# One store of eight PSUM banks for all stages, and a planner that knows of the port that VectorE and GpSimd share: a Fourier mixing layer followed by a SoLU layer on one core

## The chip, the cores and the metric

The kernel runs on one core of one Trainium2 chip. The metric is the device time of one execution in microseconds, as the median of the runs shown. The engines are called PE (TensorE), DVE (VectorE), ACT (ScalarE), POOL (GpSimd) and SP (SyncE, which issues the DMAs).

## What is computed

The input `x` has 8 images of 3136 tokens with 256 features. The first half mixes the tokens by a Fourier transform along the tokens, a complex 256x256 product with soft thresholding at 0.01, and the inverse transform. The second half takes the 25088 resulting tokens through a layer with 1024 hidden features:

```python
X = np.fft.rfft(x, axis=1)
Yr = Xr @ w_r - Xi @ w_i + b_r
Yi = Xr @ w_i + Xi @ w_r + b_i
Yr = np.sign(Yr) * np.maximum(np.abs(Yr) - lam, 0.0)
Yi = np.sign(Yi) * np.maximum(np.abs(Yi) - lam, 0.0)
y = np.fft.irfft(Y, n=x.shape[1], axis=1)
...
h = x @ w_in
e = np.exp(h - h_max)
sm = e / (np.sum(e, axis=-1, keepdims=True) + 1e-09)
solu = h * sm
ln = (solu - mu) / np.sqrt(var + 1e-06) * g_ln
return (ln @ w_out).astype(np.float32)
```

Each fp32 product is made of three fp16 products (a high and a low half of each side).

## The kernel before, in words

**The front, for each image.** 3136 tokens are 98 x 32, and the transform is done in two steps. `fwd1` (L549; `fwd1_first` at L574 for image 0) reads `x` in eight chunks `xt`, splits each into `xh` (ACT) and `xl` (DVE), multiplies by the 98-point matrix and writes `av` to DRAM. Ahead of it `load_peak` (L501) reads the image once more and takes its largest absolute value on DVE (`peaks`). `fwd2` (L626) does the 32-point step for 13 units and splits the result into `Xh` and `Xl`. `mix` (L714) multiplies by the weights (`yt`), clips (`yc`, on DVE), subtracts (`y`, on POOL) and splits again (`yh` on ACT, `yl` on POOL). `inv1` (L735) and `inv2` (L783) go back, through DRAM, into a ring of tokens in SBUF, `ring_hi` and `ring_lo`.

**The layer, for each of 196 tiles of 128 tokens.** `moe_head` (L816) makes two halves of 512 hidden features. Each half is six matmuls into one PSUM bank `ph`, whose maximum DVE takes (`nm`). From both maxima come the short columns `m`, `c` and `ch`; then ACT writes `u`, the exponential of `ph`, and DVE multiplies it by `ph` in place (also a row `u`). That last row frees the bank. POOL adds up the sums (`se`, `total`, `a`). `moe_turn` (L860) splits `u` into `lh` (ACT) and `ll` (POOL), has both transposed by DMA into `th` and `tl`, and forms the factor `r` in three POOL steps from ACT's sum of squares (`junk`). `moe_tail` (L880) multiplies `th` and `tl` by `wout` into one bank `po`; ACT scales it by `r` into `o`, which frees the bank, and one to three DMAs write `o` out.

**PSUM.** The eight banks are split into three pools (L427 to L429): three banks `ph` for heads, one bank `po` for tails, four banks `pf` for the front. Only image 0's front may use all, in a fixed turn by `front_psum` (L433), and some tiles of the last image borrow a `pf` bank (`spare`).

**What sets the order.** The kernel records every operation in a `Plan` (L222), with its engine, what it needs and a key that says which stage is due first. `weigh` (L281) gives each operation a length from constants (L228 to L231). `order` (L314) then runs through the program: for each engine it takes, among the operations that can start first, the one with the smallest key, and notes when the engine is free and when a PSUM or SBUF buffer comes free (`may_start`, L334). The order that comes out is the one in which each engine gets its instructions; on the chip they run in that order, with semaphores. The stages of one image's tiles are planned beside `front_a` (`load_peak` and `fwd1`) of the next-but-one image and `front_b` (`fwd2`, `mix`, `inv1`) of the next. As the plan records everything, all instructions carry one source line, L312.

Of the kernel before, what the change touches and what calls it, by code (L numbers as in the profile page):

```python
# [12 lines left out]
F32 = mybir.dt.float32  # L13
# [84 lines left out]
class View:  # L98
# [3 lines left out]
    def __init__(self, tile, rows, cells, dtype, path=()):  # L102
        self.tile, self.rows, self.cells, self.dtype, self.path = tile, rows, cells, dtype, path
# [61 lines left out]
class Tile:  # L165


    def __init__(self, pool, kind, shape, dtype, kw):
        self.pool, self.kind, self.shape, self.dtype, self.kw = pool, kind, shape, dtype, kw
        self.ap, self.writes, self.reads, self.users, self.owner = None, [], [], set(), None  # L170
# [20 lines left out]
class Kind:  # L191


    def __init__(self, bufs, free):
        self.bufs, self.free, self.placed, self.freed = bufs, free, [], []


class Pool:
    def __init__(self, pool, bufs, dram=False, free=False):
        self.pool, self.bufs, self.dram, self.free, self.kinds = pool, bufs, dram, free, {}  # L200

    def tile(self, shape, dtype, name, bufs=None):
        kind = self.kinds.setdefault(name, Kind(bufs or self.bufs, self.free))
        t = Tile(self.pool, kind, shape, dtype, dict(name=name, **({"bufs": bufs} if bufs else {})))
        if self.dram:
            return DramView(t)
        return View(t, (0, shape[0]), np.arange(int(np.prod(shape[1:]))).reshape(shape[1:]), dtype)


class Op:  # L210
    def __init__(self, engine, key, seq):
        self.engine, self.key, self.seq = engine, key, seq
        self.calls, self.length, self.moved, self.tiles = [], 0.0, 0.0, []
        self.needs, self.next, self.start, self.end, self.half = set(), [], None, None, False

# [6 lines left out]
class Plan:  # L222
# [91 lines left out]
    def order(self):  # L314
        ready = {e: [] for e in self.ENGINES}
        free = dict.fromkeys(self.ENGINES, 0.0)
        waits, bus, half = {}, 0.0, False
        for op in self.ops:
# [9 lines left out]
        for t, op in sorted(((t, min(t.users, key=lambda op: op.seq)) for t in left), key=lambda x: (x[1].key, x[1].seq)):  # L328
            if not t.kind.free:
                turn[t] = turns.get(t.kind, 0)  # L330
                turns[t.kind] = turn[t] + 1
        done = []

        def may_start(op):  # L334
            at = max(free[op.engine], op.at)
            for t in op.tiles:
                if t.owner is None:
                    k = t.kind
                    if turn.get(t, len(k.placed)) != len(k.placed):
                        return np.inf  # L340
                    n = len(k.placed) - k.bufs
                    if n >= 0:
                        at = max(at, k.freed[n] if n < len(k.freed) else np.inf)
            return at

        while len(done) < len(self.ops):
# [19 lines left out]
            op.start = at  # L366
            op.end = free[e] = at + op.length
            if op.moved:
                bus = max(bus, op.end) + op.moved
                op.end = bus + 2000.0  # L370
            for t in op.tiles:
                if t.owner is None:
                    t.owner = op
                    t.kind.placed.append(t)
                left[t] -= 1
                if not left[t]:
                    insort(t.kind.freed, max(o.end + self.SEEN[o.engine] for o in t.users))
            for o in op.next:
# [29 lines left out]
def fft_mix_solu_kernel(ctx: ExitStack, tc, x, w_r, w_i, b_r, b_i, w_in, w_out, g_ln, fa, fa16, fb, fs, gb, gs, ia, out):  # L408
# [22 lines left out]
    turns = [0]  # L431

    def front_psum(b):  # L433

        pool, name = ps_f, "pf"
        if b == 0:
            turns[0] += 1
            if turns[0] % 8 == 0:
                pool, name = ps_o, "po"
            elif turns[0] % 2 == 0:  # L440
                pool, name = ps_h, "ph"
        return pool.tile([P, HF], F32, name=name)

# [339 lines left out]
    def inv2(b, g):  # L783
# [5 lines left out]
        for eh in range(ND):  # L789
            pa = ps_f.tile([P, HF], F32, name="pf")  # L790
            nc.reserve(*(ring[:, eh, to : to + z - a] for ring in (ring_hi, ring_lo) for a, z, to in ((0, first, j0), (first, n, 0)) if z > a))
# [23 lines left out]

    def moe_head(k, spare):  # L816
        j = (2 * k[0] * S + k[1] * P) % R
# [3 lines left out]
        for h in range(2):  # L821
            cs = slice(h * HF, (h + 1) * HF)
            p = ps_f.tile([P, HF], F32, name="pf") if spare else ps_h.tile([P, HF], F32, name="ph")
            n = 0
            with nc.together():
                for dh in range(ND):
                    for lh, rh in ((hi, win_hi), (hi, win_lo), (lo, win_low)):
                        nc.tensor.matmul(p, lh[:, dh], rh[:, dh, cs], start=n == 0, stop=n == 3 * ND - 1)
                        n += 1
            m = sp.tile([P, 1], F32, name="nm")  # L830
            nc.vector.tensor_reduce(m, p, AX.X, ALU.max, negate=True)
            ph.append(p)
            nm.append(m)
# [45 lines left out]

    def moe_tail(k, parts, r, spare=False):  # L880
# [22 lines left out]

    pw = ps_o.tile([P, HF], F32, name="po")
    with nc.together():
# [95 lines left out]
    def power_of_two(peaks, un, sc, k):  # L1001

        top = sp.tile([P, 1], F32, name="wpeak", bufs=2)
        nc.vector.tensor_reduce(top, peaks, AX.X, ALU.max)
        pw = ps_f.tile([P, HF], F32, name="pf")
        nc.tensor.transpose(pw[:1, :P], top, ident)
# [3 lines left out]
        nc.vector.tensor_scalar(top.bitcast(U32), top.bitcast(U32), 0x7F800000, None, ALU.bitwise_and)  # L1010
        pw = ps_f.tile([P, HF], F32, name="pf")
        nc.tensor.matmul(pw[:, :1], ones[:1], top, start=True, stop=True)
# [15 lines left out]
    def finish_w_out(wo_s):  # L1028
# [10 lines left out]
        for half in wo_s[2:]:  # L1039
            nc.vector.tensor_tensor(total, total, half, op=ALU.add)  # L1040
        pw = ps_f.tile([P, HF], F32, name="pf")
        with nc.together():
# [51 lines left out]
    for b in range(B):  # L1094
# [9 lines left out]
        for n, t in enumerate(tiles):  # L1104
            need = min((t + 1) * P - (b % 2) * S, S)
            while groups < N2 // G2 and groups * G2 * N1 < need:
                nc.key = first + n - 2
                inv2(b, groups)
                groups += 1

            nc.key = first + n
            heads.append(moe_head((b // 2, t), b == B - 1 and n == 0))
# [3 lines left out]
            moe_tail(*turned.pop(0), b == B - 1 and n > L - 3 and n % 2 == 0)  # L1116
        while groups < N2 // G2:
# [28 lines left out]
```

## Time and profile before

| | us |
|---|---|
| median of 3 runs | 1732.97 |
| lowest and highest run | 1728.72, 1737.52 |
| the profiled execution, whole | 1739.42 |
| its span, first to last instruction | 1737.6 |

The mean granted clock of TensorE over the span is 0.974. The page gives each engine's busy time and its share of the span. In the tables of windows each row is a stretch of 100 us, with the busy time and the count of instructions of PE, PE's weight loads, DVE, ACT and POOL, then the granted clock, the share of the DMA engines and their GB/s. In the tables of waits a row names the waiting engine and its output tile, then the engine and output tile that it waited for, the sum in us, the number of waits and the longest. A row of the timeline has its start, its length, the engine, and the output and inputs.

### The profile page before, as it was taken

Reading aid. Unit: us, or ns where it says so; the run is one execution under the profiler, and the core shown is the slowest. Engines: PE = TensorE matmul, PEld = TensorE weight load, DVE = VectorE, ACT = ScalarE, POOL = GpSimd, SP = SyncE. Lnnn points to the kernel's source line nnn. Section 1 sums busy time; section 2 is a strip of 40 time slices with the busy share of each in tenths; the row PEclk is TensorE's granted clock in tenths of the full one; section 3 lists DMA queues with packets and bytes.
Section 4 is the critical chain, followed back from the end, with each engine's and each line's share of the span. In section 5 each row is a group of like instructions: output and inputs, shape, how many; then the busy total and the mean of one; then the engine's idle time right before and its main releaser. Section 6 shows DMA issues by size and latency. Waiting matters only on the chain.

```text
span 1737.6 us, 38336 instructions
## 1 busy us (share of the span) xinstructions
PE 1606.1 (92%) x13220; PEld 1123.6 (65%) x13220; DVE 1432.0 (82%) x3399; ACT 1251.4 (72%) x2511; POOL 1146.1 (66%) x1889
## 2 busy tenths in 40 slices
PE   5868898989999999999999899998999999999998
PEld 3435576657775677656676577765776667776665
DVE  4899978988889878997789888898789868786775
ACT  3567766776777667787678777777677768777776
POOL 1465575657776577767686577765777668776765
PEclk8888999999999999999999999999999999999999
DMA  7638974797559966799657997679856886658866
GB/s 214 223 100 207 258 172 112 193 243 155 124 131 204 237 122 134 163 225 212 128 128 162 242 195 147 122 191 234 158 133 138 176 174 143 144 106 157 137 125 113
DMA packets 531268, 290.25 MB, mean 167 GB/s; under 512 B 425758, under 2 KB 502016, under 8 KB 531072
## 3 DMA queue, kind: packets, MB, share of 16 engines
q1 hardware_dynamic: 531072, 287.80, 75.3%
q8 instruction: 103, 1.69, 0.4%
q14 instruction: 93, 0.76, 0.1%
HBM read 107.88 MB, written 77.07 MB: 106 GB/s over the span
## 4 chain that ended last, share of the span: by engine, by line
PE 57%; DVE 19%; DMA 7%; issue 6%; ACT 6%; POOL 5%; SPq 0%; DVEq 0%; ACTq 0%; POOLq 0%
PE po L312 20%; PE ph L312 20%; PE pf L312 17%; DVE u L312 4%; DMA th<-lh 2%; DVE nm L312 2%; DMA tl<-ll 2%; DVE xl L312 2%; POOL ll L312 2%; ACT u L312 2%; DVE av L312 1%; DVE yt L312 1%; ACT lh L312 1%; ACT junk L312 1%; POOL y L312 1%
## 5 line engine op out<-in xcount | busy, mean ns | idle before, releaser
L312 POOL TENSOR_TENSOR ll<-u,lh 128x1024 f16<-128x1024 f32 x196 | 430.2, 2195 | 134.8 <-ACT lh L312 128.9
L312 PE MATMUL po<-wout,th 128*128 128x256 f16 x3120 | 377.5, 275 | 14.2 <-DMA th<-lh 11.8
L312 DVE TENSOR_REDUCE nm<-ph 128x1 f32<-128x512 f32 x390 | 265.8, 685 | 134.5 <-PE ph L312 131.9
L312 PEld LDWEIGHTS <-th 128*128 128x128 f16 x3136 | 305.8, 99 | 85.5 <-DMA th<-lh 18.9
L312 ACT ACTIVATE u<-ph,m,hsb 128x512 f32<-128x512 f32 x384 | 295.0, 774 | 79.5 <-DVE m L312 78.7
L312 PE MATMUL ph<-win_hi,ring_hi 128*128 128x512 f16 x780 | 299.3, 384 | 41.1 <-DVE u L312 40.8
L312 DVE SCALAR_TENSOR_TENSOR u<-ph,ch,u 128x512 f32<-128x512 f32 x390 | 280.2, 747 | 26.7 <-ACT u L312 13.2
L312 PE MATMUL ph<-win_low,ring_lo 128*128 128x512 f16 x780 | 299.4, 384 | 0.3 <-DVE ring_lo L312 0.3
L312 PE MATMUL ph<-win_lo,ring_hi 128*128 128x512 f16 x780 | 299.4, 384 | 0.0
L312 PEld LDWEIGHTS <-ring_hi 128*128 128x128 f16 x1568 | 151.2, 99 | 180.3 <-issue 60.6
L312 ACT CAST lh<-u 128x1024 f16<-128x1024 f32 x196 | 205.1, 1047 | 83.5 <-DVE u L312 82.3
L312 ACT ACTIVATE junk<-u,total 128x1024 bf16<-128x1024 f32 x196 | 225.5, 1150 | 14.5 <-POOL total L312 14.4
L312 PE MATMUL po<-wout,tl 128*128 128x256 f16 x1560 | 202.4, 273 | 2.7 <-DMA tl<-ll 2.7
L312 PEld LDWEIGHTS <-tl 128*128 128x128 f16 x1568 | 151.1, 98 | 41.3 <-DMA tl<-ll 6.2
L312 PE MATMUL pf<-w_hi,Xl 128*128 128x256 f16 (+2 forms) x550 | 150.4, 273 | 3.0 <-DVE Xl L312 3.0
L312 ACT ACTIVATE o<-po,r 128x256 f32<-128x256 f32 x195 | 92.1, 472 | 84.4 <-PE po L312 73.1
L312 PE MATMUL pf<-w_hi,Xh 128*128 128x256 f16 (+2 forms) x550 | 150.7, 274 | 1.2 <-ACT Xh L312 0.9
L312 POOL TENSOR_TENSOR yl<-y,yh 128x512 f16<-128x512 f32 (+1 forms) x104 | 126.5, 1216 | 36.3 <-ACT yh L312 35.1
L312 PE MATMUL pf<-w_lo,Xh 128*128 128x256 f16 (+2 forms) x550 | 150.3, 273 | 0.0
L312 POOL TENSOR_TENSOR y<-yt,yc 128x512 f32<-128x512 f32 (+1 forms) x104 | 135.1, 1299 | 22.8 <-ACT yt L312 11.0
L312 PEld LDWEIGHTS <-ring_lo 128*128 128x128 f16 x784 | 77.2, 98 | 95.9 <-issue 3.8
L312 PEld LDWEIGHTS <-Xh 128*128 128x128 f16 (+1 forms) x1196 | 114.2, 99 | 31.4 <-issue 6.2
(199 smaller groups left out, 2996.5 us busy)
## 6 DMA issues: line engine op xcount, KB each, us to landing
xt<-in_x_dram SPq DMA_DIRECT2D x112, 392.0 KB
zt<-s SPq DMA_DIRECT2D x64, 392.0 KB
s<-av SPq DMA_DIRECT2D x56, 392.0 KB
bin<-s SPq DMA_DIRECT2D x42, 512.0 KB
s<-zout SPq DMA_DIRECT2D x42, 512.0 KB
out_dram<-o SPq DMA_DIRECT2D x64, 98.0 KB
u<-in_x_dram SPq DMA_DIRECT2D x8, 392.0 KB
th<-lh SPq DMA_TRANSPOSE x196
```

The source lines that it names most:

```text
L312: getattr(engine, name)(*args, **kw)
```

## The change

The three PSUM pools become one store, `Banks`, of eight banks. Each PSUM tile has a kind with a limit of its own: `pf` (front) 5, `ph` (heads) 5, `po` (tails) 2, and `pb` (image 0's front) 8. A tile may start when its kind is below its limit and any bank of the store is free; the plan takes the bank that comes free first and gives the tile that bank by name. The `spare` cases go.

The planner's lengths change, and it gets one more resource: an operation that uses the port (every POOL operation, DVE's `tensor_scalar` and `tensor_copy` on SBUF alone, and DVE's operations with two SBUF inputs and no PSUM operand) may start only when the last such operation has ended. The arithmetic and the number of instructions are not touched.

```diff
 class Tile:
     def placed(self):
         if self.ap is None:
-            self.ap = self.pool.tile(self.shape, self.dtype, **self.kw)
+            slot = {} if self.bank is None else dict(tag=f"bank{self.bank}")
+            self.ap = self.pool.tile(self.shape, self.dtype, **self.kw, **slot)
...
+class Banks:
+    def __init__(self, pool, n, **most):
+        self.pool, self.kinds = pool, {name: Kind(m, self) for name, m in most.items()}
+        self.free = [(0.0, i) for i in range(n)]
+
+    def tile(self, name):
+        t = Tile(self.pool, self.kinds[name], [128, 512], F32, dict(name=name, bufs=1))
+        return View(t, (0, 128), np.arange(512), F32)
...
-    CALL = dict(vector=58.0, scalar=52.0, gpsimd=110.0)
-    ELEMENT = dict(vector=1.07, scalar=0.83, gpsimd=2.03)
-    SCALAR = dict(vector=60.0, scalar=92.0, gpsimd=140.0)
+    CALL = dict(vector=64.0, scalar=54.0, gpsimd=140.0)
+    ELEMENT = dict(vector=1.07, scalar=0.83, gpsimd=1.93)
+    SCALAR = dict(vector=60.0, scalar=92.0, gpsimd=120.0)
...
-            op.length += 1500.0 if cross else 430.0
+            op.length += 1600.0 if cross else 430.0
...
-            op.length += self.CALL[op.engine] + big * self.ELEMENT[op.engine] + max(scalars, 0) * self.SCALAR[op.engine]
+            each = self.ELEMENT[op.engine]
+            wide = [v for v in ins if v.cells.size > 1]
+            sbuf = not any(v.tile.kind.banks for v in (*ins, *outs))
+            if op.engine == "scalar" and sbuf:
+                each = 0.87
+            if op.engine == "gpsimd" and len(wide) == 2 and all(v.dtype == F32 for v in (*wide, *outs)):
+                each = 2.12
+            if op.engine == "vector" and sbuf and name in ("tensor_scalar", "tensor_copy") and big > 1:
+                each, op.port = 0.545, True
+            if op.engine == "vector" and sbuf and len(wide) == 2:
+                op.port = True
+            if op.engine == "gpsimd":
+                op.port = True
+            op.length += self.CALL[op.engine] + big * each + max(scalars, 0) * self.SCALAR[op.engine]
...
         def may_start(op):
-            at = max(free[op.engine], op.at)
+            at = max(free[op.engine], op.at, port if op.port else 0.0)
+            taken = {}
...
-                    n = len(k.placed) - k.bufs
+                    n -= k.bufs
                     if n >= 0:
                         at = max(at, k.freed[n] if n < len(k.freed) else np.inf)
+                    if k.banks is not None:
+                        n, spare = taken.get(k.banks, 0), k.banks.free
+                        taken[k.banks] = n + 1
+                        at = max(at, spare[n][0] if n < len(spare) else np.inf)
...
             op.end = free[e] = at + op.length
+            if op.port:
+                port = op.end
...
+                    if t.kind.banks is not None:
+                        t.bank = t.kind.banks.free.pop(0)[1]
...
-    ps_h = Pool(ctx.enter_context(tc.tile_pool(name="ps_h", bufs=3, space=PSUM)), 3, free=True)
-    ps_o = Pool(ctx.enter_context(tc.tile_pool(name="ps_o", bufs=1, space=PSUM)), 1, free=True)
-    ps_f = Pool(ctx.enter_context(tc.tile_pool(name="ps_f", bufs=4, space=PSUM)), 4, free=True)
+    banks = Banks(ctx.enter_context(tc.tile_pool(name="ps", bufs=1, space=PSUM)), 8, pf=5, ph=5, po=2, pb=8)
...
-            p = ps_f.tile([P, HF], F32, name="pf") if spare else ps_h.tile([P, HF], F32, name="ph")
+            p = banks.tile("ph")
...
-        po = ps_f.tile([P, HF], F32, name="pf") if spare else ps_o.tile([P, HF], F32, name="po")
+        po = banks.tile("po")
```

The change moves instructions on every engine. Two places follow, both at the 97th of the 196 tiles; the numbers tell tiles of one name apart.

On DVE, before: the rows from the tile's `m` to the two `u` that free its banks `ph_15034` and `ph_15087`; `av` and `peaks` belong to the next-but-one image's front.

```order
L312 TENSOR_SCALAR m_15129<-nm_15074,nm_15117,hsb_5288 128x1
L312 SCALAR_TENSOR_TENSOR av_15127<-pf_15102,av_15127 98x2x256
L312 TENSOR_SCALAR c_15145<-m_15129 128x1
L312 SCALAR_TENSOR_TENSOR av_15127<-pf_15113,av_15127 98x2x256
L312 TENSOR_SCALAR c_15145<-c_15145 128x1
L312 TENSOR_REDUCE peaks_15019<-xt_15030 128x1
L312 RECIPROCAL c_15145<-c_15145 128x1
L312 TENSOR_REDUCE nm_15161<-ph_15135 128x1
L312 TENSOR_SCALAR ch_15168<-c_15145,hsb_5288 128x1
L312 TENSOR_REDUCE peaks_15019<-xt_15045 128x1
L312 SCALAR_TENSOR_TENSOR u_15142,su0_15175<-ph_15034,ch_15168,u_15142 128x512
L312 SCALAR_TENSOR_TENSOR u_15142,su1_15189<-ph_15087,ch_15168,u_15142 128x512
```

On DVE, now: the same stretch of the same tile, whose banks are `ph_14813` and `ph_14975`.

```order
L339 TENSOR_SCALAR m_15033<-nm_14850,nm_15008,hsb_7262 128x1
L339 SCALAR_TENSOR_TENSOR av_15017<-pf_15003,av_15017 98x2x256
L339 TENSOR_SCALAR c_15049<-m_15033 128x1
L339 SCALAR_TENSOR_TENSOR av_15017<-pf_15012,av_15017 98x2x256
L339 TENSOR_SCALAR c_15049<-c_15049 128x1
L339 TENSOR_REDUCE nm_15072<-ph_15021 128x1
L339 RECIPROCAL c_15049<-c_15049 128x1
L339 TENSOR_REDUCE nm_15076<-ph_15037 128x1
L339 TENSOR_SCALAR ch_15081<-c_15049,hsb_7262 128x1
L339 TENSOR_REDUCE peaks_15083<-xt_14966 128x1
L339 SCALAR_TENSOR_TENSOR u_15046,su0_15097<-ph_14813,ch_15081,u_15046 128x512
L339 SCALAR_TENSOR_TENSOR u_15046,su1_15101<-ph_14975,ch_15081,u_15046 128x512
```

Before, one half of the next tile (`nm_15161`) has its maximum taken ahead of this tile's `u`, so three head banks are in use. Now both halves of the next tile (`nm_15072`, `nm_15076`) are there, so four are, and one of the two `peaks` stands elsewhere.

On POOL, before: the rows from the tile's `ll` to the next tile's `a`.

```order
L312 TENSOR_TENSOR ll_15210<-u_15142,lh_15204 128x1024
L312 TENSOR_SCALAR r_15250<-var_15208,a_15165 128x1
L312 TENSOR_TENSOR r_15250<-r_15250,mhalf_92 128x1
L312 TENSOR_TENSOR r_15250<-r_15250,unscale_1306 128x1
L312 TENSOR_TENSOR se0_15248<-se0_15248,se1_15258 128x1
L312 TENSOR_SCALAR a_15278<-se0_15248,c_15254 128x1
```

On POOL, now: the same stretch.

```order
L339 TENSOR_TENSOR ll_15142<-u_15046,lh_15114 128x1024
L339 TENSOR_SCALAR r_15177<-var_15131,a_15079 128x1
L339 TENSOR_TENSOR se0_15150<-se0_15150,se1_15165 128x1
L339 TENSOR_TENSOR r_15177<-r_15177,mhalf_86 128x1
L339 TENSOR_SCALAR a_15193<-se0_15150,c_15126 128x1
L339 TENSOR_TENSOR r_15177<-r_15177,unscale_1291 128x1
```

The next tile's `se` and `a` now stand between the three steps of this tile's `r`, which came in one piece before.

More of the change, by code (lines that the diff above doesn't have):

```diff
@@ L169, in __init__ @@
         self.pool, self.kind, self.shape, self.dtype, self.kw = pool, kind, shape, dtype, kw
[L170 removed]
+        self.ap, self.writes, self.reads, self.users, self.owner, self.bank = None, [], [], set(), None, None
     def placed(self):
         if self.ap is None:
[L174 removed]
+            slot = {} if self.bank is None else dict(tag=f"bank{self.bank}")
+            self.ap = self.pool.tile(self.shape, self.dtype, **self.kw, **slot)
         return self.ap
@@ L191, with __init__ @@
 class Kind:
-    def __init__(self, bufs, free):
-        self.bufs, self.free, self.placed, self.freed = bufs, free, [], []
+    def __init__(self, bufs, banks):
+        self.bufs, self.banks, self.placed, self.freed = bufs, banks, [], []
 class Pool:
-    def __init__(self, pool, bufs, dram=False, free=False):
-        self.pool, self.bufs, self.dram, self.free, self.kinds = pool, bufs, dram, free, {}
+    def __init__(self, pool, bufs, dram=False):
+        self.pool, self.bufs, self.dram, self.kinds = pool, bufs, dram, {}
     def tile(self, shape, dtype, name, bufs=None):
-        kind = self.kinds.setdefault(name, Kind(bufs or self.bufs, self.free))
+        kind = self.kinds.setdefault(name, Kind(bufs or self.bufs, None))
         t = Tile(self.pool, kind, shape, dtype, dict(name=name, **({"bufs": bufs} if bufs else {})))
@@ L213, in __init__ @@
         self.calls, self.length, self.moved, self.tiles = [], 0.0, 0.0, []
-        self.needs, self.next, self.start, self.end, self.half = set(), [], None, None, False
+        self.needs, self.next, self.start, self.end, self.half, self.port = set(), [], None, None, False, False
     def touch(self, tile):
@@ L316, in order @@
         free = dict.fromkeys(self.ENGINES, 0.0)
-        waits, bus, half = {}, 0.0, False
+        waits, bus, half, port = {}, 0.0, False, 0.0
         for op in self.ops:
@@ L328, in order @@
         for t, op in sorted(((t, min(t.users, key=lambda op: op.seq)) for t in left), key=lambda x: (x[1].key, x[1].seq)):
-            if not t.kind.free:
+            if t.kind.banks is None:
                 turn[t] = turns.get(t.kind, 0)
@@ L374, in order @@
                     t.kind.placed.append(t)
+                    if t.kind.banks is not None:
+                        t.bank = t.kind.banks.free.pop(0)[1]
                 left[t] -= 1
                 if not left[t]:
-                    insort(t.kind.freed, max(o.end + self.SEEN[o.engine] for o in t.users))
+                    freed = max(o.end + self.SEEN[o.engine] for o in t.users)
+                    insort(t.kind.freed, freed)
+                    if t.kind.banks is not None:
+                        insort(t.kind.banks.free, (freed, t.bank))
             for o in op.next:
@@ L426, in fft_mix_solu_kernel @@
     sp = Pool(ctx.enter_context(tc.tile_pool(name="sp", bufs=4)), 4)
-    ps_h = Pool(ctx.enter_context(tc.tile_pool(name="ps_h", bufs=3, space=PSUM)), 3, free=True)
-    ps_o = Pool(ctx.enter_context(tc.tile_pool(name="ps_o", bufs=1, space=PSUM)), 1, free=True)
-    ps_f = Pool(ctx.enter_context(tc.tile_pool(name="ps_f", bufs=4, space=PSUM)), 4, free=True)
-    turns = [0]
+    banks = Banks(ctx.enter_context(tc.tile_pool(name="ps", bufs=1, space=PSUM)), 8, pf=5, ph=5, po=2, pb=8)
     def front_psum(b):
[L435 to L442, printed above, removed]
+        return banks.tile("pf" if b else "pb")
     def load(shape, src, name, pool=const, dtype=F32, **kw):
@@ L789, in inv2 @@
         for eh in range(ND):
-            pa = ps_f.tile([P, HF], F32, name="pf")
+            pa = banks.tile("pf")
             nc.reserve(*(ring[:, eh, to : to + z - a] for ring in (ring_hi, ring_lo) for a, z, to in ((0, first, j0), (first, n, 0)) if z > a))
@@ L900, in moe_tail @@
             j += n
-    pw = ps_o.tile([P, HF], F32, name="po")
+    pw = banks.tile("po")
     with nc.together():
@@ L1004, in power_of_two @@
         nc.vector.tensor_reduce(top, peaks, AX.X, ALU.max)
-        pw = ps_f.tile([P, HF], F32, name="pf")
+        pw = banks.tile("pf")
         nc.tensor.transpose(pw[:1, :P], top, ident)
@@ L1010, in power_of_two @@
         nc.vector.tensor_scalar(top.bitcast(U32), top.bitcast(U32), 0x7F800000, None, ALU.bitwise_and)
-        pw = ps_f.tile([P, HF], F32, name="pf")
+        pw = banks.tile("pf")
         nc.tensor.matmul(pw[:, :1], ones[:1], top, start=True, stop=True)
@@ L1040, in finish_w_out @@
             nc.vector.tensor_tensor(total, total, half, op=ALU.add)
-        pw = ps_f.tile([P, HF], F32, name="pf")
+        pw = banks.tile("pf")
         with nc.together():
@@ L1111, in fft_mix_solu_kernel @@
             nc.key = first + n
-            heads.append(moe_head((b // 2, t), b == B - 1 and n == 0))
+            heads.append(moe_head((b // 2, t)))
             nc.key = first + n + 0.5
@@ L1115, in fft_mix_solu_kernel @@
             nc.key = first + n + 1
-            moe_tail(*turned.pop(0), b == B - 1 and n > L - 3 and n % 2 == 0)
+            moe_tail(*turned.pop(0))
         while groups < N2 // G2:
```

8 lines of the change are left out of this document (5 added, 3 removed).

## The prediction

> **What bounds the kernel now.** I read the page's head first, then a table of 100 us windows, then TensorE's waits, then the timeline around its longest wait for a bank.
>
> ```profile
> span 1737.6 us, 38336 instructions
> PE 1606.1 (92%) x13220; PEld 1123.6 (65%) x13220; DVE 1432.0 (82%) x3399; ACT 1251.4 (72%) x2511; POOL 1146.1 (66%) x1889
> PE 57%; DVE 19%; DMA 7%; issue 6%; ACT 6%; POOL 5%; SPq 0%; DVEq 0%; ACTq 0%; POOLq 0%
> ```
>
> TensorE is busy for 1606.1 of 1737.6 us and carries 57% of the chain that ended last. It bounds the kernel, so a change gains only out of its 131.5 us of idle time. The change neither adds nor removes a matmul. The windows show where that idle time lies (the first columns are window, us, PE, PEld and DVE busy, each with its count).
>
> ```profile
> 0.00:100.00 100.00, 72.23 (x418) 39.04 (x418) 71.58 (x126) 50.74 (x95) 33.79 (x32) 0.85 0.63 202
> 100.00:200.00 100.00, 78.29 (x530) 47.64 (x531) 94.53 (x209) 72.81 (x139) 56.47 (x77) 0.88 0.74 187
> 300.00:400.00 100.00, 90.43 (x712) 61.45 (x710) 90.37 (x213) 73.61 (x149) 63.16 (x103) 0.97 0.91 211
> 400.00:500.00 100.00, 97.94 (x890) 73.27 (x889) 82.84 (x195) 72.49 (x149) 74.65 (x125) 1.00 0.63 138
> 500.00:600.00 100.00, 92.47 (x704) 60.18 (x702) 87.19 (x209) 75.68 (x152) 60.23 (x107) 0.97 0.89 204
> 600.00:700.00 100.00, 97.40 (x894) 74.29 (x892) 78.64 (x180) 69.69 (x145) 75.15 (x116) 0.98 0.67 131
> 900.00:1000.00 100.00, 92.61 (x720) 61.75 (x719) 89.75 (x214) 77.51 (x152) 62.53 (x108) 0.98 0.86 194
> 1500.00:1600.00 100.00, 98.55 (x853) 70.30 (x851) 78.36 (x207) 74.51 (x158) 71.39 (x130) 1.00 0.70 132
> ```
>
> The first 200 us hold 49.5 us of it, at a granted clock of 0.85 and 0.88. After that windows alternate. Where the next-but-one image is read and transformed (300, 500, 900), VectorE is at 87 to 90% and TensorE loses 7 to 10 us. In the others TensorE loses about 2. What it waits for there:
>
> ```profile
> PE ph L312 <- DVE u L312: 40.8, 37, 2.9
> PE po L312 <- DMA th<-lh: 11.8, 12, 2.6
> PE po L312 <- DMA tl<-ll: 2.7, 5, 1.0
> PE po L312 <- ACT o L312: 2.4, 4, 1.0
> PE pf L312 <- DMA th<-lh: 1.3, 1, 1.3
> ```
>
> The largest entry is a head half that finds no free `ph` bank: 40.8 us in 37 waits. The longest of them, from the timeline:
>
> ```profile
> 970.62 0.38 PE L312 MATMUL ph<-win_hi,ring_hi 128*128 128x512 f16 x1
> 970.84 0.38 PE L312 MATMUL ph<-win_lo,ring_hi 128*128 128x512 f16 x1
> ...
> 971.18 0.68 DVE L312 SCALAR_TENSOR_TENSOR av<-pf,av 98x512 f16<-98x512 f32 x1
> ...
> 972.89 0.97 DVE L312 TENSOR_REDUCE peaks<-xt 128x1 f32<-128x784 f32 x1 [0.98 <-DMA xt<-in_x_dram]
> ...
> 975.44 0.74 DVE L312 SCALAR_TENSOR_TENSOR u<-ph,ch,u 128x512 f32<-128x512 f32 x1
> ...
> 976.24 0.38 PE L312 MATMUL ph<-win_hi,ring_hi 128*128 128x512 f16 x1 [2.86 <-DVE u L312]
> ```
>
> VectorE stood behind a late load (0.98 us), so the `u` that frees a head's bank ran at 975.44, and TensorE sat for 2.86 us. The `av` of 971.18 had by then emptied one of the four `pf` banks, which a head may not use. The first two rows also show that matmuls start 0.22 us apart though a row reads 0.38. Idle time counts from the end of that row, so each wait costs some 0.16 us more than its figure.
>
> **The change, part by part.**
>
> *A. Heads may hold five banks of the store instead of three.* The 37 waits cost 40.8 + 37 x 0.16 = 47 us. I counted in the order what TensorE does between the end of a head's matmuls and the next use of that bank, in steps of the 0.22 us between two matmuls. From the second image on, the least is 3.4 us before and 5.5 after; a twentieth lie under 5.1 before and under 7.2 after. Where only a tenth of the heads wait now, a longer distance at the short end should end most waits. But the wait above had 7.7 us of such work and still came, since VectorE was late. I take three quarters: -35 (bounds 0 and -47).
>
> *B. Two tails may be open.* The tail's waits for its transposed halves are 11.8 + 2.7 + 1.3 = 15.8 us in 18 waits, with the 0.16 each 19 us. TensorE's work between a tile's head and its tail grows: nine tenths had over 10.4 us before, and 11.1 after. The tail's output DMAs and the two transposes of each tile move with it on SyncE's queue; their number is the same. I take half: -9 (bounds +5 and -19). The wait for `o`, 2.4 us in 4, was never much although one bank served every tail.
>
> *C. VectorE and GpSimd hold each other off.* First what that costs (groups, then the two tiles' minimum/median/maximum in ns, then one clash):
>
> ```profile
> L312 DVE SCALAR_TENSOR_TENSOR xl<-xt,sc,xh 98x1024 f16<-98x1024 f32 x56 | 92.1, 1646 | 2.5 <-ACT xh L312 2.3
> L312 DVE TENSOR_SCALAR yc<-yt,sc 128x512 f32<-128x512 f32 x84 | 83.1, 990 | 1.4
> ```
>
> ```profile
> L312 DVE SCALAR_TENSOR_TENSOR xl<-xt,sc,xh x56: 1256/1282/3189, 157.3 to 1380.1; 98x1024 f16<-98x1024 f32 x56
> ```
>
> ```profile
> L312 DVE TENSOR_SCALAR yc<-yt,sc x91: 529/673/2448, 231.7 to 1547.2; 128x512 f32<-128x512 f32 x84, 64x512 f32<-64x512 f32 x7
> ```
>
> ```profile
> 546.35 2.12 POOL L312 TENSOR_TENSOR ll<-u,lh 128x1024 f16<-128x1024 f32 x1 [1.30 <-ACT lh L312]
> ...
> 546.49 3.05 DVE L312 SCALAR_TENSOR_TENSOR xl<-xt,sc,xh 98x1024 f16<-98x1024 f32 x1
> ...
> 548.45 1.23 POOL L312 TENSOR_SCALAR r<-var,a 128x1 f32<-128x1 f32 x1
> ```
>
> `xl` needs 1.26 us when left alone and took 3.05 while GpSimd's `ll` ran; then GpSimd's next row took 1.23. Over the run that is 56 x (1646 - 1256) ns = 22 us and 84 x (990 - 529) ns = 39 us, together 61 us of VectorE. The Trainium skill ("SBUF — State Buffer", Who interferes with whom) says that such a pair is locked for a whole instruction, and that issue order, not the kind of operation, decides who blocks; by that, a list of numbers in a planner cannot remove a clash, only shift it; this term would be 0 and the sum -30. The rows agree that either side can be held. By the planner's view, with a quarter of the clashes gone, the term would be -15 and the sum -45, as VectorE's time is worth about its own length only in the busy windows. I take 0 (bounds +10, as every operation is moved, and -15), so that A is not counted twice.
>
> *D. The front shares the store.* With five banks at heads and two at tails one is left for the front, which had four. No row of before shows a front tile that waits for a bank because of a head. Bounds: 0, and the heads' own rate of 37 waits in 392 halves (two for each of 196 tiles) at 1.1 + 0.16 us each, over the 650 or so front groups that the order holds: 61 x 1.26 = 77 us. The order leaves the front's banks as long as before (median 6 to 8 us of TensorE's work from one use to the next), so I take +5, near the low end.
>
> *E. VectorE is next.* Of A's 35 us I put two thirds into the windows with VectorE at 87 to 94%. Two of them alone hold 14.6 of the 40.8 us (100 to 200, then 900 to 1000):
>
> ```profile
> PE ph L312 <- DVE u L312: 7.4, 6, 2.9
> ```
>
> ```profile
> PE ph L312 <- DVE u L312: 7.2, 5, 2.9
> ```
>
> There a bank more only lets TensorE run ahead until VectorE is behind by as much again. I take half of those two thirds back: +12 (bounds 0 and +25).
>
> *F. The start.* The order puts four groups of the next image's first transform (12 matmuls at 0.22 us, 2.6 us) ahead of the first `inv2`, where TensorE idles: -3 (bounds 0 and -8). For image 0 all eight banks were in use before too.
>
> Sum: -35 - 9 + 0 + 5 + 12 - 3 = -30 us. The profiled execution took 1739.42 us; 1709.4 is its counterpart. The median of the runs, 1732.97, lies 6.4 us under that execution, so I forecast **1703 us**.
>
> **The rivals.** About 0.5%, 8.7 us, can be told from no change, that is below 1724.3 or above 1741.6.
>
> *More.* A and B go whole, and a quarter of the clashes: -47 - 19 - 15 - 3 + 5 = -79, 1654 us. For it: five banks cover the whole wait shown. Against it: VectorE at 90% where the waits are.
>
> *VectorE takes it all.* A's last third (-12), B -9 and F -3 stay and E and D return 20: -4, 1729 us. For it: alternating windows where TensorE's share falls as VectorE's rises. Against it: 5 to 10% of VectorE is still idle there.
>
> *Slower: the tails hold up the heads.* A tail's bank is freed by ScalarE's `o`, which needs GpSimd's `r`. In the new order GpSimd does the next tile's `se` amid the three steps of `r`, and `se` waits for the next tile's `u`:
>
> ```profile
> POOL se L312 <- ACT u L312: 118.9, 95, 5.0
> ```
>
> That is 1.25 us each time. Before, a late `o` could stop only the next tail; now a head or front group may stand next in that bank, and all of TensorE's queue behind it. At 1.25 + 0.16 us it would take 33 tails of 196 to eat A, B and F (47 us). If half of the tails do so, 98 x 1.41 = 138 us come in and 47 go: 1824 us; at a quarter, 69 - 47 = +22 us, 1755 us, which I take. Against it: the new order leaves nine tenths of the tails' banks over 3.2 us, against 1.3 before, where the wait for `o` was 2.4 us in all.
>
> **How the numbers follow.** Forecast 0.58, its own range 1685 to 1722 (A between half and all, D to +15); more 0.15; VectorE takes it all 0.15; slower 0.12. Faster by over 0.5%: 0.58 + 0.15 + 0.03 of the third case = 0.76. Within it: the other 0.12. Slower: 0.12. The range reaches from 1672, half way into the case of more, to 1738, past the third case, and leaves out some 0.08 below and 0.12 above.
>
> **What would show it.** TensorE's wait for `u` under 12 us, and for `th` and `tl` under 9; TensorE's share in the windows at 300, 500 and 900 up from 90 to 93% to 94% or more with VectorE at 92% or more. If those windows show no rise though the waits for `u` are gone, E was too small. A total of waits for `o` over 20 us would show the slower case. Mean `yc` under 800 ns would show that C was worth more than 0.

## The result, and the profile after

The changed kernel takes 1663.8 us in the median of four runs (1657.7 to 1667.3), the kernel before 1733.8. The ratio is 0.959, with a 95% interval of 0.956 to 0.963. The forecast was 1703 us with a range of 1672 to 1738, so the gain of 70 us is more than double the 30 us that were forecast, and the time lies under the range.

The profiled execution took 1657.7 us, the shortest of the four, while the one of before, at 1739.4 us, is longer than the four counted here (1728.7 to 1737.5). So the two profiles lie 81.8 us apart where the medians lie 70.0 apart. The page begins:

```profile
span 1655.8 us, 38277 instructions
PE 1581.2 (95%) x13220; PEld 1116.7 (67%) x13220; DVE 1381.2 (83%) x3399; ACT 1244.9 (75%) x2511; POOL 1134.9 (69%) x1889
PE 73%; DVE 8%; DMA 8%; ACT 4%; POOL 3%; issue 3%; SPq 0%; DVEq 0%; ACTq 0%; POOLq 0%
```

TensorE is still the bound, and more clearly: 73% of the chain instead of 57%. Its idle time fell from 131.5 to 1655.8 - 1581.2 = 74.6 us. VectorE did the same work in 51 us less (1432.0 to 1381.2). The 59 instructions fewer in all are of none of these four engines, whose counts are the same. After the first 200 us, the window of before that lost most is one that the prediction did not show, first below. Then five windows of after whose counterparts it showed:

```profile
200.00:300.00 100.00, 89.19 (x807) 66.50 (x806) 83.32 (x186) 65.56 (x135) 67.41 (x99) 0.97 0.68 161
```

```profile
100.00:200.00 100.00, 81.24 (x553) 49.23 (x553) 91.11 (x207) 72.75 (x142) 54.57 (x79) 0.88 0.65 164
300.00:400.00 100.00, 97.13 (x802) 68.22 (x800) 91.54 (x221) 80.25 (x162) 70.12 (x123) 1.00 1.01 218
400.00:500.00 100.00, 100.00 (x901) 74.37 (x898) 82.02 (x199) 70.91 (x144) 75.56 (x115) 1.00 0.65 142
500.00:600.00 100.00, 95.91 (x769) 66.12 (x768) 89.45 (x228) 82.27 (x167) 67.34 (x122) 0.98 0.99 218
900.00:1000.00 100.00, 97.07 (x819) 69.84 (x818) 88.42 (x217) 81.73 (x167) 69.28 (x124) 1.00 1.01 220
200.00:300.00 100.00, 97.83 (x923) 74.64 (x922) 84.06 (x209) 75.06 (x155) 75.48 (x115) 1.00 0.80 177
```

In the windows at 300, 500 and 900 TensorE went from 90 to 93% up to 96 or 97%, and the granted clock from 0.97 or 0.98 to 1.00 in two of the three. VectorE's share hardly moved there, though more instructions ran. In the window at 200 TensorE lost 10.8 us, not about 2, with VectorE at only 83%; three waits of the front (4.5, 1.4 and 0.7 us), of the kind shown further down, make 6.5 of them. The first 200 us hardly gained: 48.4 us of idle time against 49.5. TensorE's waits:

```profile
PE po L339 <- DMA tl<-ll: 6.5, 9, 1.5
PE po L339 <- DMA th<-lh: 4.5, 6, 1.3
PE pf L339 <- DVE u L339: 3.2, 6, 1.4
PE po L339 <- DVE u L339: 2.1, 2, 1.1
PE pf L339 <- ACT o L339: 1.0, 1, 1.0
PE ph L339 <- DVE u L339: 0.2, 1, 0.2
```

The heads' wait for a bank went from 40.8 us to 0.2. The new kinds of wait, a front tile behind a head's `u` or a tail's `o`, come to 4.2 us; a tail's tile behind a `u`, new as well, adds 2.1.

Where the 81.8 us of the span went: 56.9 are idle time. Of these 40.9 are the heads' (the group of their first matmuls, 41.1 us of idle before and 0.2 after), 16.3 the front's own (next rows) and 4.8 the tails' waits for `th` and `tl`. That makes 62.0, and 5.1 came back elsewhere: in the first 200 us the heads had lost 7.4 us, yet that stretch as a whole gained only 1.1. A second loss lies in the clock: over windows of 2 us, 2 us x (1 - granted clock) adds up, after the first 200 us, to 17.1 us before and 2.3 after, so 14.8. The third is the end of each wait: TensorE's waits after 200 us went from 74 to 32, at 0.16 us each 6.7. These last two fit the fall of TensorE's busy time, 1606.1 - 1581.2 = 24.9 us. Together with the idle time that is 78.4 of 81.8 us. The clock's share is on the high side: this profile of before has a mean clock of 0.974, and the runs of before beside the experiments 0.974 to 0.979.

The front's own part is in the inverse transform, of which each step (`inv1`) needs two banks at once. Its matmuls by shape after the first 200 us, before and then after:

```profile
L312 PE MATMUL pf<-yh,gb 64*128 64x256 f16 x672 | 65.7, 278 | 16.4 <-DVE Xs L312 4.5 <-DVE yt L312 3.7 <-DVE Xl L312 3.7
```

```profile
L339 PE MATMUL pf<-yh,gb 64*128 64x256 f16 x672 | 58.1, 271 | 0.1
```

(The page's row over the whole run has 19.5 us before, but 3.1 of them are image 0's, whose tiles are called `pb` now and are not in the row of after.) The releasers `Xs`, `yt` and `Xl` do not make `yh`; they are the readers of other `pf` banks. One such wait, from the timeline of before:

```profile
740.42 0.28 PE L312 MATMUL pf<-yh,gb 64*128 64x256 f16 x1
742.70 0.39 PE L312 MATMUL pf<-yh,gb 64*128 64x256 f16 x3 [2.00 <-DVE av L312]
```

The first matmul has its data and its bank. The second, into the pair's other bank, waits 2.00 us for `av` to leave it. Nine of the ten waits in the row of before are of this kind, at the second matmul of a step; the longest, at 284.95 us, is 4.46 us, behind `Xs`.

The clock's part shows behind the wait at 976 us that the prediction quoted. Windows of 2 us of before, with the granted clock third from the end of the row, and the timeline of the same place:

```profile
974.00:976.00 2.00, 0.00 (x0) 0.00 (x0) 2.00 (x4) 0.60 (x1) 0.46 (x2) 1.00 0.71 174
976.00:978.00 2.00, 1.76 (x5) 0.64 (x5) 1.46 (x5) 1.11 (x2) 0.19 (x1) 0.63 1.12 329
978.00:980.00 2.00, 2.00 (x10) 1.23 (x9) 1.26 (x2) 1.56 (x3) 1.99 (x1) 0.51 0.85 298
980.00:982.00 2.00, 2.00 (x15) 1.34 (x14) 1.68 (x7) 1.48 (x4) 1.13 (x4) 1.00 0.97 254
```

```profile
977.22 0.63 PE L312 MATMUL ph<-win_hi,ring_hi 128*128 128x512 f16 x1
977.64 0.63 PE L312 MATMUL ph<-win_lo,ring_hi 128*128 128x512 f16 x1
978.07 0.63 PE L312 MATMUL ph<-win_low,ring_lo 128*128 128x512 f16 x1
```

After the wait the matmuls start 0.43 us apart instead of 0.22, for some 3.3 us: 2 x (0.37 + 0.49) = 1.7 us on top of the wait. Before there were nine such places after the first 200 us and ahead of the last few (the one behind the 4.46 us lasts twice as long); after, one. Three of the nine stand behind waits of the front's pairs. The one of after stands behind two waits close together, both of the new kinds:

```profile
532.76 0.59 PE L339 MATMUL pf<-xh,fa_s 98*98 98x512 f16 x2 [0.96 <-ACT o L339]
534.95 0.85 PE L339 MATMUL pf<-xh,fa_s 98*98 98x512 f16 x2 [1.38 <-DVE u L339]
```

### The profile page after: what moved, and what is told of

Its sections match the earlier page's. It is cut to its first block, busy times and chain, and to the rows that moved or that the text cites. A ratio compares the mean times of both kernels' runs of the same rounds, so it can differ in the third digit from the quotient of the medians.

```text
span 1655.8 us, 38277 instructions
## 1 busy us (share of the span) xinstructions
PE 1581.2 (95%) x13220; PEld 1116.7 (67%) x13220; DVE 1381.2 (83%) x3399; ACT 1244.9 (75%) x2511; POOL 1134.9 (69%) x1889
## 4 chain that ended last, share of the span: by engine, by line
PE 73%; DVE 8%; DMA 8%; ACT 4%; POOL 3%; issue 3%; SPq 0%; DVEq 0%; ACTq 0%; POOLq 0%
PE po L339 25%; PE ph L339 24%; PE pf L339 22%; DMA tl<-ll 2%; DMA th<-lh 2%; PE pb L339 2%; DVE u L339 1%; POOL ll L339 1%; DMA xt<-in_x_dram 1%; DVE yt L339 1%; DMA u<-in_x_dram 1%; DVE nm L339 1%; DMA zt<-s 1%; ACT u L339 1%; ACT junk L339 1%
## 5 line engine op out<-in xcount | busy, mean ns | idle before, releaser
L339 POOL TENSOR_TENSOR ll<-u,lh 128x1024 f16<-128x1024 f32 x196 | 425.4, 2170 | 113.5 <-ACT lh L339 107.8
L339 ACT ACTIVATE junk<-u,total 128x1024 bf16<-128x1024 f32 x196 | 226.5, 1155 | 14.8 <-POOL total L339 14.6
L339 POOL TENSOR_TENSOR y<-yt,yc 128x512 f32<-128x512 f32 (+1 forms) x104 | 139.0, 1337 | 44.0 <-DVE yc L339 36.8
L339 POOL TENSOR_TENSOR yl<-y,yh 128x512 f16<-128x512 f32 (+1 forms) x104 | 127.8, 1229 | 49.5 <-ACT yh L339 47.2
L339 PE MATMUL pf<-w_hi,Xl 128*128 128x256 f16 (+1 forms) x546 | 148.9, 273 | 1.1 <-DVE Xl L339 1.0
L339 PE MATMUL pf<-w_hi,Xh 128*128 128x256 f16 (+1 forms) x546 | 149.3, 273 | 0.6 <-DVE u L339 0.6
L339 PE MATMUL pf<-w_lo,Xh 128*128 128x256 f16 (+1 forms) x546 | 148.9, 273 | 0.0
```

Of the source, the lines that this page charges most:

```text
L339: getattr(engine, name)(*args, **kw)
```

## The experiments

Two theories stood against each other. S: the store is most of the gain. P: the planner with the port is most of it, as VectorE loses less to GpSimd. Each group of runs has runs of the kernel before beside it, whose medians lay between 1729.9 and 1733.6 us; the ratios are to these.

**The two halves alone**, each in two plans: as it is, and with 2 ns more for every VectorE call in the planner, which should change nothing but the plan. `e1` and `e18` keep the store and take the old planner; `e2` and `e17` keep the three old pools and take the new one. In short, against the changed kernel (the other lengths go back with the first line of `e1`):

```diff
 e1, e18:
-    CALL = dict(vector=64.0, scalar=54.0, gpsimd=140.0)
+    CALL = dict(vector=58.0, scalar=52.0, gpsimd=110.0)    (e18: vector=60.0)
...
-            at = max(free[op.engine], op.at, port if op.port else 0.0)
+            at = max(free[op.engine], op.at)
 e2, e17:
-    banks = Banks(..., 8, pf=5, ph=5, po=2, pb=8)
+    ps_h, ps_o, ps_f = pools of 3, 1 and 4 banks           (e17: vector=66.0)
```

> The store of eight banks alone, planned with the old lengths and without the port. Theory S (the store gives most: the heads' 40.8 us of waits for a bank, the waits inside the inverse transform's pairs, and the slow-clock stretches of 1.7 us behind each long wait go with it): 1675 to 1695 us, TensorE's wait of ph for u under 5 us, at most three slow-clock stretches after 200 us, while yc stays near 990 ns and xl near 1646 ns. Theory P (the planner gives most: VectorE is the bound in every other window and the 40 us of hold-off that it no longer has are the gain): 1710 to 1728 us, with waits for VectorE that only have other names.

> The new lengths and the port alone, with the three old pools of 3, 1 and 4 banks. Theory S: 1705 to 1728 us; ph still waits for u for 20 us or more although yc falls to about 830 ns. Theory P: 1675 to 1695 us, the wait of ph for u falls under 15 us without a bank more.

> The new lengths and the port with the three old pools and the same 2 ns, a second plan of that kind beside 1701 us. If the planner alone brings some 30 us: 1694 to 1709 us. If luck: 1720 us or more, or under 1690.

> The store with the old lengths and no port, with 2 ns more for each VectorE call, a second plan of that kind beside 1674 us. If the store alone brings some 56 us: 1667 to 1681 us. If luck: under 1664 or above 1690 us.

| | median us | ratio to before, 95% |
|---|---|---|
| store alone (e1, e18) | 1673.5, 1673.4 | 0.967 (0.965 to 0.970), 0.965 (0.962 to 0.967) |
| planner alone (e2, e17) | 1701.3, 1705.9 | 0.984 (0.982 to 0.987), 0.984 (0.981 to 0.987) |

The store alone brings 56 and 60 us and the planner alone 29 and 28. S holds for the larger part, but P is no small thing: `e1` and `e2` lie just under the ranges that S gave (1675 to 1695 and 1705 to 1728 us), while `e17` and `e18` repeat them, and the two gains together are more than the 70 us of the whole change, so they overlap. Other signs of S were missed by a little: `e1` has four slow places instead of at most three, and `yc` and `xl` fell to 951 and 1494 ns although its planner knows of no port. Waits of `ph` for `u` in `e1` and in `e2`:

```profile
PE ph L326 <- DVE u L326: 1.6, 2, 1.1
```

```profile
PE ph L325 <- DVE u L325: 31.6, 24, 3.2
```

As S said, the planner alone leaves most of that wait standing. What it gains lies elsewhere: `yc` falls to 726 ns there, the slow clock after 200 us costs 5.7 us instead of 17.1, and the waits of the front's pairs become fewer though its four banks are the same (7.0 us over the whole run, against 19.5):

```profile
L325 PE MATMUL pf<-yh,gb 64*128 64x256 f16 x720 | 71.3, 272 | 7.0 <-DVE Xs L325 2.3 <-ACT yh L325 1.9 <-DVE ring_lo L325 1.6
```

**The port rule taken out** (`e3`; `e15` with the 2 ns): the changed kernel, in whose plan operations on the port may overlap.

```diff
-            at = max(free[op.engine], op.at, port if op.port else 0.0)
+            at = max(free[op.engine], op.at)
```

> The changed kernel with the new lengths, but its planner lets operations on the shared port overlap. Theory S: 1664 to 1676 us, yc back to 900 ns or more and xl to 1550 or more, while PE's waits stay as short as in the changed kernel. Theory P: 1685 to 1710 us.

> The store and the new lengths without the port, with 2 ns more for each VectorE call, a second plan of that kind beside 1676 us. If the port is worth some 15 us of its own: 1668 to 1684 us, above all plans that have store and port (1649 to 1664). If the 12 us were a plan's luck: 1650 to 1664 us.

They took 1675.9 us (0.969, 0.967 to 0.972) and 1664.7 us (0.960, 0.956 to 0.963); the second lies between its two ranges. The groups of the changed kernel, and then of `e3`:

```profile
L339 DVE SCALAR_TENSOR_TENSOR xl<-xt,sc,xh 98x1024 f16<-98x1024 f32 x56 | 79.6, 1426 | 0.9 <-ACT xh L339 0.6
L339 DVE TENSOR_SCALAR yc<-yt,sc 128x512 f32<-128x512 f32 x84 | 70.0, 834 | 0.9
```

```profile
L339 DVE SCALAR_TENSOR_TENSOR xl<-xt,sc,xh 98x1024 f16<-98x1024 f32 x56 | 95.1, 1698 | 2.7 <-ACT xh L339 2.4
L339 DVE TENSOR_SCALAR yc<-yt,sc 128x512 f32<-128x512 f32 x84 | 84.1, 1002 | 1.1
```

In `e3` the hold-off of before is back (990 and 1646 ns there), in `e15` in part (927 and 1511). In every plan with the rule `yc` has a mean of 683 to 834 ns, and in every plan without it, before included, 927 to 1002. So an order does take clashes away; from before to the changed kernel it is 84 x 156 ns + 56 x 220 ns = 25 us on these two rows. The Trainium skill ("SBUF — State Buffer", Who interferes with whom) lets issue order decide who blocks. The clash that the prediction quoted agrees: `ll` started 0.14 us ahead of `xl` and kept to 2.12 us, while `xl` took 3.05 instead of 1.26. But that an order can only shift a clash, as the prediction read it, does not follow. In time, the two plans without the rule have a mean of 1670 us and the two with it (1663.8, and `e13` below) one of 1657. With scatter as below, 13 us is a guess of the size, not more.

**The limits of the store.** The changed kernel with other limits: `e4` those of the old pools, `e5` three heads (`e16` with the 2 ns), `e6` one tail, `e7` none, `e10` six, six and three. The expectations set theory A, the prediction's (heads gain because they may hold five banks), against theory R (each group takes, of all eight banks, the one that has rested longest).

```diff
-    banks = Banks(..., 8, pf=5, ph=5, po=2, pb=8)
+    e4: pf=4, ph=3, po=1    e5, e16: pf=5, ph=3, po=2    e6: pf=5, ph=5, po=1
+    e7: pf=8, ph=8, po=8    e10: pf=6, ph=6, po=3        (pb=8 in all)
```

> The changed kernel with the limits of the old pools on the new store (pf 4, ph 3, po 1; image 0 may use 8). Theory S, read as a matter of how many banks a stage may hold: 1705 to 1728 us, as the plan alone. If what matters is that any bank may serve any stage, or by theory P: 1664 to 1680 us.

> The changed kernel with at most three heads' banks in the plan instead of five. Theory R (what ends the heads' waits is that every group takes, of all eight banks, the one that has rested longest; the limit of heads hardly matters): 1660 to 1672 us, wait of ph for u under 5 us. Theory A, the prediction's (it is the five banks that heads may hold): 1678 to 1692 us, wait of ph for u 15 us or more.

> Three heads' banks with the same 2 ns, a second plan of that kind beside 1682 us. If the heads' limit matters by some 20 us: 1672 to 1690 us. If it was luck: 1650 to 1664 us.

> The changed kernel with one tail's bank in the plan instead of two. Theory R with the second tail as the other part: 1678 to 1692 us, near the 1689 of the old limits, with 20 us or more of TensorE's waits for th and tl. Theory A: 1662 to 1674 us, those waits at most 16 us.

> The changed kernel without limits: each kind may hold all eight banks. Theory R: 1655 to 1672 us, since heads that run ahead only take rested banks. If heads that run ahead starve the front, as the limits of five and two suggest: 1672 to 1700 us, with new waits of pf groups for u and o.

> The changed kernel with limits of six for the front, six for heads and three for tails. Theory R: 1655 to 1670 us, and TensorE's waits for th and tl at most the 11 us of the changed kernel. If the limits of five and two are where front and layer balance: 1670 to 1690 us.

| limits pf, ph, po | median us | ratio to before, 95% |
|---|---|---|
| 4, 3, 1 (e4) | 1689.0 | 0.977 (0.975 to 0.978) |
| 5, 3, 2 (e5, e16) | 1681.6, 1689.0 | 0.970 (0.969 to 0.972), 0.974 (0.970 to 0.977) |
| 5, 5, 1 (e6) | 1649.5 | 0.952 (0.950 to 0.954) |
| 8, 8, 8 (e7) | 1658.8 | 0.958 (0.956 to 0.960) |
| 6, 6, 3 (e10) | 1654.9 | 0.955 (0.954 to 0.957) |

The heads' limit matters, by more than 17 us; the others do not show. Neither theory came out whole: `e5` and `e16` have the time that A gave and the short wait that R gave, `e4` lies between its two ranges, `e6` under both of its, `e7` in R's and `e10` at its lower end. TensorE's waits in `e5`, and then the one of `ph` in `e4`:

```profile
PE po L339 <- DMA th<-lh: 12.9, 11, 2.3
PE po L339 <- DMA tl<-ll: 4.2, 3, 1.9
PE ph L339 <- DVE u L339: 0.4, 1, 0.4
```

```profile
PE ph L339 <- DVE u L339: 1.5, 1, 1.5
```

With three heads the wait for `u` is as good as gone too. `e2` and `e4` make the cleanest pair, as they have the same planner and the same limits, once as pools and once in one store: the wait falls from 31.6 to 1.5 us. (Their times, 1701.3 and 1689.0 us, are too near each other to size this by one plan each.) The limit exists only in the plan; on the chip a head waits for the last reader of its own bank, and with eight banks in one store that bank has rested for long. Counted in the order as in the prediction, a twentieth of the heads' banks are used again within 5.1 us of TensorE's work before, and only after more than 7 us in the changed kernel and in `e5` alike. What three heads cost shows as tails that wait for `th` and `tl` (17.1 us in `e5` and 23.6 in `e16`, against 11.0), and as more slow clock (8.5 and 9.2 us against 2.3 after 200 us). That this is all of it is not shown.

**How far plans scatter** (`e13`: the changed kernel with the 2 ns; `e14`: the same with one tail).

```diff
-    CALL = dict(vector=64.0, scalar=54.0, gpsimd=140.0)
+    CALL = dict(vector=66.0, scalar=54.0, gpsimd=140.0)
```

> The changed kernel with 2 ns more for each VectorE call in the planner, which should mean nothing on the chip: it shows how far the time moves between plans that are equally good. If plans scatter: a change of 6 to 15 us either way. If the time follows the limits of the store: within 5 us of the changed kernel.

> One tail's bank instead of two, with the same 2 ns. If one tail is truly better than two: again 8 to 18 us under the plan with two tails and the same 2 ns. If the 14 us were a plan's luck: within 6 us of it or above.

They took 1650.8 us (0.952, 0.950 to 0.954) and 1660.6 us (0.958, 0.956 to 0.960). The 2 ns moved the changed kernel by 13 us and turned the sign of the comparison of one tail with two. So the one-tail kernel at 1649.5 us beats both kernels, but as one plan among equals: the six plans with store, port rule and five heads or more lie between 1649 and 1664 us, and the changed kernel is the slowest of them.

**Waits put in** (`e11`, `e12`). Theory C says that a wait itself brings the slow clock behind it. At 22 heads TensorE does a small matmul, ScalarE then copies its operand one or five times, and TensorE needs the copy for a second small matmul. The copies are of a tile of zeros that serves nothing else.

```diff
+   self.nc.tensor.matmul(p[:, :128], s[:, :128], s[:, :128], start=True, stop=True)
+   for _ in range(5):                      # e11: 1
+       self.nc.scalar.copy(s, s)
+   self.nc.tensor.matmul(p[:, :128], s[:, :128], s[:, :128], start=True, stop=True)
```

> The changed kernel, in which TensorE is made to wait at 22 heads for one small ScalarE copy (the copied tile is used for nothing). Theory C (a wait of some 2 us or more puts TensorE's granted clock to 0.5 for 3.3 us, 1.7 us lost on top of the wait): waits of 1 to 2 us, so few slow stretches, at most 8 after 200 us, and +20 to +45 us on the changed kernel. Rival (a wait costs its own length alone and the slow stretches come from elsewhere): one slow stretch after 200 us as in the changed kernel, +18 to +30 us.

> The same with five copies behind each other, so waits of 3 to 4.5 us at 22 heads. Theory C: a slow stretch behind nearly each, 18 to 24 after 200 us, and 60 to 100 us of waits plus some 37 us of slow clock over the changed kernel. Rival: the waits alone, and at most three slow stretches.

`e11` took 1678.4 us (0.968, 0.966 to 0.970), 14.7 us over the changed kernel and so under both of its ranges; `e12` took 1767.7 us (1.020, 1.018 to 1.023). The waits that were put in, in `e11` and in `e12`:

```profile
PE ph L345 <- ACT probe L344: 20.3, 22, 2.6
```

```profile
PE ph L345 <- ACT probe L344: 77.0, 22, 4.9
```

Windows of 2 us of `e12` around one of them:

```profile
762.00:764.00 2.00, 0.87 (x5) 0.29 (x3) 1.89 (x7) 1.97 (x4) 0.99 (x5) 1.00 0.63 151
764.00:766.00 2.00, 0.00 (x0) 0.00 (x0) 1.70 (x4) 1.90 (x4) 0.19 (x1) 0.99 0.93 190
766.00:768.00 2.00, 1.82 (x6) 0.72 (x7) 0.00 (x0) 2.00 (x3) 0.85 (x1) 0.50 0.94 290
768.00:770.00 2.00, 2.00 (x8) 0.81 (x7) 0.87 (x2) 0.24 (x3) 1.92 (x3) 0.66 1.04 271
```

In `e12` 18 of the 22 waits are followed by such a stretch, some by two in a row; the slow clock after 200 us costs 45.0 us against 2.3. In `e11`, with 0.9 us a wait, only the one of 2.6 us is. Theory C holds: the wait makes the slow stretch, and the small matmuls do not, since `e11` has them too. Over the changed kernel's span `e12` has 108.6 us more; its waits and slow clock make 77 + 43 = 120, so some 11 us were taken up by slack elsewhere.

## Why the prediction was wrong, point by point

The direction, the bound and the largest term's row were right. The sum, -30 us against a measured -70, was too small by more than half. Five steps failed: A was taken too small and for another reason than the one that counts, C and a term for the clock were put at nothing, D had the wrong sign, and E took back what VectorE did not take. Numbers here are those of the two profiles, which lie 82 us apart.

*A, -35.* The wait went whole: -41 us of idle and 37 x 0.16 = 6 more, the term's own bound. The reason given, five banks for heads, is not what ended it: `e5` has three and `e4` the limits of the old pools, and the wait is gone in both. It is the shared store, in which a bank rests longer. Five banks are still worth 17 us or more in time, by a way that stays open.

*B, -9.* The waits measured -4.8 us, without their ends. A second tail is not what brought it: one tail and two cannot be told apart.

*C, 0.* The clashes fell by 25 us on the two rows it named, and VectorE by 51 us in all. Of the 51 us, 32 and 21 went with the store alone as well (1399.9 us in `e1`, 1410.9 in `e18`). The rule is worth about 13 us on top of the store, a guess of the size; the planner as a whole brings 28 with the three pools, where fewer waits of the front's pairs and less slow clock carry much of it. The prediction held C at 0 so as not to count A twice.

*D, +5, bounds 0 and +77.* This had the wrong sign, and its bounds left out a gain: the front's own waits fell by 16.3 us, against 4.2 us of new ones. "No row of before shows a front tile that waits for a bank because of a head" was true and beside the point: the front waited for the front. The row of `yh,gb` with 19.5 us stood in the profile, among the groups by shape. So did the longest wait for a bank after the start: not the 2.86 us quoted but the front's 4.46.

*E, +12.* VectorE took nothing back that shows: in the busy windows TensorE reached 96 to 97% with VectorE at 88 to 92%. That holds even where VectorE kept most of its clashes: the store alone gained 56 us with `yc` at 951 ns.

*F, -3.* The first 200 us gained 1.1 us of idle time.

*What no term had.* A wait was priced at its length and 0.16 us. The long ones cost 1.7 us more by the clock, 14.8 us in all. The rows of the quoted wait went on to show it, and the quote stopped at the row where the wait ended. The windows' clock of 0.97 and 0.98 was read as a given.

With A at -47, the front at -16, the clock at -15, E at 0, and B and F as they were, the same working gives -90 us, against -82 in the profile. The case called more (1654 us, 0.15) came nearest: A went whole as it says, but the front and the clock, which it leaves out, made the rest. In the rival where VectorE takes it all, E and D as forecast return 12 + 5 = 17 us, not 20, and E's 12 are already in what A loses there; that rival's 1729 us and the upper end of the range, set past it, hang on this, and nothing else.

*The signs.* The wait for `u` (0.2 us) and TensorE's windows (96 to 97%) passed theirs, though VectorE was at 88 to 92% where 92% or more was named. The waits for `th` and `tl`, 11.0 us, missed their 9. The slower case's sign, waits for `o`, was 1.0 us. Mean `yc`, 834 ns, stayed over the 800 that would have shown C to be worth something, and yet C was; most other plans with the rule lie under it.

## What to carry to other kernels

Where stages share a resource in fixed parts, look for the waits inside each part as well as those of the largest user: here a stage that needs two buffers at once waited for its own part. Price a wait of the bound engine by the rows after it, too. Before two planned orders are compared, nudge the planner by something that means nothing, since two plans that differ by 2 ns in one constant lay up to 13 us apart here, as much as the port rule was worth.

## What was not expected of the hardware

A single wait of 1.6 to 2.9 us halves TensorE's granted clock for about 3.3 us, often but not always: of the waits over 2.2 us before, all five after the start did so, of those between 1.5 and 2.2 us four of 13. It need not be one wait: the place left in the changed kernel has 0.96 and 1.38 us with 0.8 us of matmuls between them. The Trainium skill ("TensorE: Matmul & The Clock Gate", HAM oscillation — how this bites in real kernels) warns of gaps over about 3.4 us; here less than half of that was enough. The same page of the Trainium skill (What's actually happening) gives a free-running window of that length, which fits the stretch of 3.3 us and that equal waits of 3.31 us in `e12` were followed by a slow stretch in most cases and not in four. The clock can go with the time of a run as well: the changed kernel's shortest run has a mean clock of 0.982 and its longest, 9.6 us longer, 0.975, and 0.007 of 1660 us is 11.6 us. That is not general: the shortest and the longest run of `e16`, 9.2 us apart, both show 0.978.
